# Entering the attention core of a two-block training kernel: the row shift by Ln and Exp, its last quarter inside the core, and q's second half stored in four pieces

## The chip, the cores and the metric

The kernel runs on one core of a Trainium2 chip. The metric is the time of one execution in microseconds, read on the device. Nine runs of the kernel before gave a median of 1085.01 us (1078.76 to 1089.26).

## The reference

Two small attention blocks are run forward and backward on 2048 tokens of width 448 with 16 heads of 28. Block A is linear attention, block B has one key and value head for all 16 query heads. The outputs are the forward result of both and all eight gradients. What matters here is block B:

```python
q = (x @ wq).reshape(B, S, H, Dh).transpose(0, 2, 1, 3)
k, v = x @ wk, x @ wv
p = softmax(einsum("bhqd,bkd->bhqk", q, k) * Dh ** -0.5)
o = einsum("bhqk,bkd->bhqd", p, v)
out_B = o.transpose(0, 2, 1, 3).reshape(B, S, H * Dh) @ wo
_out, _vjp = jax.vjp(_fwd, A_x, ..., B_wo)
_grads = _vjp(grad_out)
```

A softmax may subtract any number of its own from each row. The kernel subtracts the bound |q| * max|k|, the square root of |q|^2 * max|k|^2, which is called the shift. It is stored as row 0 of each head's group of 32 rows in q (28 of the others are the head's values), and k has -1 in that row, so that the matmul of q and k delivers the shifted score.

## The kernel before, in words

The program has three stages.

**Phase A** (to about 194 us) does block A. **Phase B** (`phase_B_pre`, 194 to 223 us) forms k, v and q of block B, and the shifts. **The core** (223 to about 1010 us) runs forward and backward of block B's attention together. A tail forms the remaining gradients. In the first two stages a planner orders the instructions of each engine; the core is under `tc.manual_schedule()`, where each engine's order is the program's.

Phase B goes over q in four chunks of 512 tokens (`qc`). For each, TensorE makes four groups of 128 rows (L571), ScalarE copies them into `R1`, which is `qT` (L572), VectorE squares them (L574), and TensorE sums the squares by head into `pn` (L577). Then ScalarE takes the square root with the scale `kmax2` (L579) into `shifts[qc]`, a part of the tile `ga` for the first three chunks and of `R3` for the last. Four small DMAs on GpSimd's queue write the 16 rows into `R1` (L581). After every second chunk, SyncE's queue issues four DMA transposes of 1024 tokens of `R1` into `qn` (L586; `qn` is the tile `gaT`) and one store of 1 MB to `qn_d` in DRAM (L587). The core reads `qn_d` back in an order of its own (`qX`).

The core goes over 64 blocks of 256 queries by 2 heads, each in 8 units `u` of 256 keys, so 512 units and 28 more that drain the pipeline. A unit computes scores into `sps` (two PSUM banks of three in `SB`) and exponentiates them on ScalarE into `eT` (L891 and L931). From unit 16 on the backward step of unit `u - 16` runs beside it: `dps` (two banks, `DB`) is multiplied by `eT` on VectorE (L896), and, after a copy `cp` on ScalarE (L898), on GpSimd (L899), which gives `dsT`. Every fourth unit, one DMA transpose on SyncE's queue makes `eN` from four units of `eT` (L933, 1 MB). The gradient of v (`dv_mm`) reads `eN` from unit 20 on. The gradient of k (`dk_m`) reads `qX` from unit 27 on. The 256 KB of `qX` that a range of 8 blocks needs come in four loads on GpSimd's queue (L904), where `a` is a group of 32 partitions: for the first range at units 10, 14, 18 and 22, for the second at 34, 42, 50 and 58. In units 1 to 15 TensorE also projects the output gradient (`do_proj`, evicted on VectorE at L866).

Memory is taken from pools. `cA` holds nearly all working tiles of phases A and B (`xa`, `ga`, `pq`, `ppB` and others), `cB` only `gaT`, `awk` some small ones, and `psA` the eight PSUM banks, four each under the names `aacc` and `agen`. All four close at L605, and the core's pools are laid over the same memory: `eT`, `eN`, `dsT` and one `qX` buffer over `cA`, the other `qX` buffer (`pqb_`) over `cB`, `dsx` over both. A pool that lies over a closed one waits for it: the first instruction on each engine that touches a tile of the new pool carries the waits.

## Time and profile before

| | |
|---|---|
| median of 9 runs | 1085.01 us (1078.76 to 1089.26) |
| the profiled execution | 1085.64 us, of which the span of the trace is 1083.9 us |
| granted TensorE clock, mean over the span | 0.992 |
| busy: TensorE, ScalarE, VectorE, GpSimd | 1035.3 (96%), 875.7 (81%), 894.6 (83%), 772.4 (71%) us |
| table loads on ScalarE | three of 1.28 us: at the start, at L579 (207.5 us), at L870 (222.5 us) |
| first and last exponential of the core, L891 | start at 223.93 and 1006.97 us |
| one unit in the steady core | 1.46 us (median distance of the L891 starts) |

How to read it: a line of the profile names start, duration, engine, line, operation, output and inputs; a bracket holds the idle time of the engine before it and what ended that. TensorE's share is that of issued work and not of its peak. The program is the same in the nine runs, which are not profiled.

### The profile page before, as it was taken

To read this page: it belongs to the slowest core of one execution; us is meant where nothing else is said; L and a number is where in the kernel's file an instruction comes from. 1 tells how busy PE (TensorE), PEld (TensorE's weight loads), DVE (VectorE), ACT (ScalarE), POOL (GpSimd) and SP (SyncE) were. 2 spreads that over 40 slices of the span, in tenths; PEclk is the share of its full clock that TensorE was granted. 3 is DMA by queue.
4 is the path that set the end of the run, shared out by engine and by line. 5 is a ranking of instruction groups with operands and counts; after the bars stand their busy time and mean duration, and the time that the engine had idled before them with its cause. 6 is when DMAs were issued, how large, how long until landed. Compare 5 with 4: busy or idle time off the path is not lost.

```text
span 1083.9 us, 40115 instructions
## 1 busy us (share of the span) xinstructions
PE 1035.3 (96%) x16326; PEld 494.3 (46%) x16329; DVE 894.6 (83%) x1790; ACT 875.7 (81%) x1743; POOL 772.4 (71%) x1014
## 2 busy tenths in 40 slices
PE   9999999998999999999999999999999999999998
PEld 5555555443444444444444444444444444444434
DVE  6887400437999999999999999999999999999942
ACT  6453122577999999999999999999999999999621
POOL 6001143226888888889888888988988899888881
PEclk9999999989999999999999999999999999999999
DMA  9869899399999999999999999999999999999973
GB/s 237 161 124 195 166 188 213 63 212 160 200 185 195 199 209 190 191 192 195 195 179 191 197 197 190 203 187 187 187 205 186 191 198 189 192 180 180 224 133 90
DMA packets 669026, 199.36 MB, mean 184 GB/s; under 512 B 646008, under 2 KB 664736, under 8 KB 668840
## 3 DMA queue, kind: packets, MB, share of 16 engines
q1 hardware_dynamic: 656296, 175.23, 97.0%
q0 software_dynamic: 7584, 17.59, 6.8%
q10 hardware_dynamic: 4960, 3.96, 1.3%
q8 instruction: 128, 2.10, 0.8%
q14 instruction: 58, 0.48, 0.1%
HBM read 20.99 MB, written 12.94 MB: 31 GB/s over the span
## 4 chain that ended last, share of the span: by engine, by line
PE 39%; ACT 19%; POOL 15%; DVE 13%; issue 10%; DMA 4%; ACTq 0%; DVEq 0%; POOLq 0%; SPq 0%
PE agen L81 13%; POOL dsT L899 11%; ACT cp L898 10%; ACT eT L931 7%; PE sps L640 6%; DVE dsx L962 5%; PE oq L640 5%; PE aacc L81 5%; DVE dsT L896 3%; PE sps L81 3%; PE dv_acc L640 2%; DMA eN<-eT 1%; PE dk_acc L640 1%; PE dps L640 1%; POOL prod L787 1%
## 5 line engine op out<-in xcount | busy, mean ns | idle before, releaser
L899 POOL TENSOR_TENSOR dsT<-cp,eT 128x512 bf16<-128x512 bf16 x512 | 588.6, 1157 | 103.2 <-ACT cp L898 97.5
L962 DVE STREAM_TRANSPOSE dsx<-dsT 128x512 f32<-128x512 f32 x512 | 357.9, 699 | 2.4 <-DVE ot L710 0.2
L640 PEld LDWEIGHTS <-R 128*32 128x32 bf16 (+1 forms) x9184 | 229.7, 94 | 276.7 <-issue 237.0
L896 DVE TENSOR_TENSOR dsT<-dps,eT 128x512 bf16<-128x512 f32 x512 | 341.8, 668 | 15.9 <-PE dps L640 11.1
L891 ACT ACTIVATE eT<-sps 128x512 bf16<-128x512 f32 x512 | 312.6, 611 | 23.4 <-PE dps L640 10.0
L898 ACT ACTIVATE cp<-dps 128x512 bf16<-128x512 f32 x512 | 314.2, 614 | 12.0 <-PE dps L640 10.9
L931 ACT ACTIVATE eT<-sps 128x512 bf16<-128x512 f32 x512 | 320.3, 626 | 0.0
L640 PE MATMUL dk_acc<-dsx,qX 32*32 32x512 bf16 x4096 | 269.4, 376 | 2.9 <-DMA qX<-qn_d 2.9
L640 PE MATMUL dps<-doT,R 32*128 32x256 bf16 x2048 | 248.4, 269 | 1.9 <-ACT cp L898 0.8
L640 PE MATMUL sps<-R,R 32*128 32x256 bf16 (+1 forms) x2240 | 222.6, 274 | 7.8 <-DVE R L866 1.7
L640 PE MATMUL oq<-eT,R 128*32 128x256 bf16 x2048 | 158.5, 276 | 0.0
L640 PE MATMUL oq<-dsT,R 128*32 128x256 bf16 x2048 | 156.9, 275 | 0.1
L640 PEld LDWEIGHTS <-qX 32*32 32x32 bf16 x4096 | 80.1, 89 | 118.5 <-issue 55.4
L640 PE MATMUL dv_acc<-eN,don 128*32 128x512 bf16 x1024 | 97.7, 381 | 1.0 <-DMA eN<-eT 1.0
L81 PEld LDWEIGHTS <-R 128*128 128x128 bf16 (+1 forms) x525 | 42.1, 100 | 40.8 <-issue 11.0
L401 POOL COPY pk<-R 128x256 bf16<-128x256 bf16 x4 | 1.6, 398 | 75.3 <-DVE R L361 66.1
L553 DVE TENSOR_TENSOR osb<-R 32x512 bf16<-32x512 bf16 x4 | 1.6, 412 | 59.0 <-ACT R L550 59.0
L640 PEld LDWEIGHTS <-don 128*32 128x32 bf16 x1024 | 33.9, 97 | 2.2 <-issue 1.6
L787 POOL TENSOR_TENSOR prod<-R,oTs 128x128 f32<-128x128 bf16 x64 | 28.0, 437 | 9.3 <-DVE oTs L783 8.9
L916 DVE TENSOR_SCALAR R<-oq 64x256 bf16<-64x256 f32 x64 | 27.3, 427 | 3.6 <-PE oq L640 1.6
L804 PE MATMUL sps<-identB,don 128*32 128x128 bf16 x256 | 18.5, 222 | 12.3 <-POOL don L796 8.0
L81 PE MATMUL agen<-R,R 128*128 128x448 bf16 x128 | 28.8, 354 | 0.2 <-ACT R L220 0.2
(223 smaller groups left out, 987.5 us busy)
## 6 DMA issues: line engine op xcount, KB each, us to landing
qX<-qn_d POOLq DMA_DIRECT2D x32, 256.0 KB, 4.6
out_dram<-osb ACTq DMA_DIRECT2D x22, 112.0 KB
qn_d<-gaT SPq DMA_DIRECT2D x2, 1024.0 KB
eN<-eT SPq DMA_TRANSPOSE x128
xa<-in_A_x_dram SPq DMA_DIRECT2D x8, 224.0 KB
ga<-in_grad_out_dram SPq DMA_DIRECT2D x4, 448.0 KB
xa<-in_grad_out_dram POOLq DMA_DIRECT2D x4, 448.0 KB, 9.0
out_dram<-wdq POOLq DMA_DIRECT2D x8, 224.0 KB, 4.5
```

What stands on the lines that cost most here:

```text
L81: nc.tensor.matmul(out_ap, lhsT=lhsT, rhs=rhs, start=start, stop=stop, tile_position=(0, 0))
L401: nc.gpsimd.tensor_copy(out=pk[:, t4, D:512], in_=gqn[:, t4, 3 * P:D])
L640: nc.tensor.matmul(out, lhsT=lhsT, rhs=rhs, start=start, stop=stop, tile_position=pos, skip_group_check=True)
L787: nc.gpsimd.tensor_tensor(out=prod[b][:], in0=dnv, in1=os_, op=ALU.mult)
L804: nc.tensor.transpose(tp2[q:q + 32, qb * P:(qb + 1) * P], don[b][:, qb, h, :], identB[:, :], tile_position=(0, q))
L891: nc.scalar.activation(out=eT(u)[:, 0, :], in_=sp[0][:, :], func=ACT.Exp, scale=scale)
L896: nc.vector.tensor_tensor(out=dst[:, 0, :], in0=dp[0][:, :], in1=ew[:, 0, :], op=ALU.mult)
L898: nc.scalar.activation(out=cp[:, :], in_=dp[1][:, :], func=ACT.Copy)
L899: nc.gpsimd.tensor_tensor(out=dst[:, 1, :], in0=cp[:, :], in1=ew[:, 1, :], op=ALU.mult)
L916: nc.vector.tensor_scalar(out=qT_B[g][64 * hp:64 * hp + 64, qc * 256:(qc + 1) * 256], in0=oq[64:128, 0:256], scalar1=scale, scalar2=None, ...
L931: nc.scalar.activation(out=eT(u)[:, 1, :], in_=sp[1][:, :], func=ACT.Exp, scale=scale)
L962: nc.vector.transpose(out=dsx[b][:, tp, :, :, :].rearrange("p h t c -> p (h t c)").bitcast(F32), in_=dsT[y][:, :, :].rearrange("p h c -> p ...
```

## The change

The square root becomes `Ln` and `Exp`: `exp(0.5 * ln(kmax2 * pn + 1e-30))`, first in place in PSUM, then into the shift. The dummy activation at the core's entry (L870) goes. For the last chunk of 512 tokens this step and its four small DMAs are moved into the core, behind the first exponential of unit 1. The first half of `qn` is kept in eight rows of `ppB` (pool `cA`) in place of `gaT` (pool `cB`). The second half is transposed at the core's start into the buffer of `qX` that lies in `pqb_`, and is stored by tokens in four pieces of 256 KB on GpSimd's queue at units 34, 42, 50 and 58; the second range of `qX`, which uses that buffer next, is loaded at units 66, 70, 74 and 78, and `wo` at 86 in place of 70. The PSUM pool `psA` stays open, and the core's banks are taken from its two names.

```diff
@@ phase_A @@
-        return xbT, wq_pad, rep, bsel, gaB, ga[:, 8:12, :]
+        return xbT, wq_pad, rep, bsel, ppB[:, 6:14, :], ga[:, 8:12, :]
@@ phase_B_pre @@
-            shift = shifts[qc]
-            nc.scalar.activation(out=shift, in_=pn[0:H, :], func=ACT.Sqrt, scale=kmax2[:, 0:1])
-            for g in range(4):
-                nc.gpsimd.dma_start(qT[:, g, qs].rearrange("(j r) s -> j r s", r=32)[:, 0, :], shift[4 * g:4 * g + 4, :])
-            if qc % 2:
-                q2 = slice((qc - 1) * 512, (qc + 1) * 512)
-                t2 = slice(4 * qc - 4, 4 * qc + 4)
+            if qc == NQC - 1:
+                break
+            q_shift(pn, shifts[qc], qs)
+            if qc == 1:
                 for g in range(4):
-                    nc.sync.dma_start_transpose(qn[:, t2, g * P:(g + 1) * P], qT[:, g, q2])
-                nc.sync.dma_start(qn_d[q2, :].rearrange("(t p) c -> p t c", p=P), qn[:, t2, :])
+                    nc.sync.dma_start_transpose(qn[:, :, g * P:(g + 1) * P], qT[:, g, 0:1024])
+                nc.sync.dma_start(qn_d[0:1024, :].rearrange("(t p) c -> p t c", p=P), qn)
+    def q_shift(pn, shift, qs):
+        nc.scalar.activation(out=pn[0:H, :], in_=pn[0:H, :], func=ACT.Ln, bias=eps[:, 0:1], scale=kmax2[:, 0:1])
+        nc.scalar.activation(out=shift, in_=pn[0:H, :], func=ACT.Exp, scale=0.5)
+        for g in range(4):
+            nc.gpsimd.dma_start(R1[:, g, qs].rearrange("(j r) s -> j r s", r=32)[:, 0, :], shift[4 * g:4 * g + 4, :])
@@ between the stages @@
+    psc = ExitStack()
+    psA = psc.enter_context(tc.tile_pool(name="psA", bufs=4, space=bass.MemoryType.PSUM))
     with ExitStack() as pa:
-        psA = pa.enter_context(tc.tile_pool(name="psA", bufs=4, space=bass.MemoryType.PSUM))
-        phase_B_pre(pa, cA, awk, psA, io)
+        last_shift = phase_B_pre(pa, cA, awk, psA, io)
-        SB = [psA.tile([P, 512], F32, name=f"sps{i}") for i in range(3)]
-        DB = [psA.tile([P, 512], F32, name=f"dps{i}") for i in range(2)]
+        SB = [psA.tile([P, 512], F32, name="aacc") for i in range(3)]
+        DB = [psA.tile([P, 512], F32, name="agen") for i in range(2)]
+        oq, dk_acc = (psA.tile([P, 512], F32, name="agen") for _ in range(2))
@@ the core's loop @@
-            tc.keep_in_program_order(nc.scalar.activation(out=ex[:], in_=ex[:], func=ACT.Exp))
+            qn = pqb_.tile([P, 8, 512], BF16, name="qX")
+            for g in range(4):
+                nc.sync.dma_start_transpose(qn[:, :, g * P:(g + 1) * P], R1[:, g, 1024:2048])
...
+                if u == 1:
+                    q_shift(*last_shift)
+                    dv_acc = psA.tile([P, 512], F32, name="aacc")
...
-                for a in {10: (0,), 14: (2,), 18: (1,), 22: (3,)}.get(u, ()) or {34: (0,), 42: (2,), 50: (1,), 58: (3,)}.get(u % 64, ()) * (u < 448):
-                    qc = u // 64 + (u > 24)
+                for n in {34: (0,), 42: (1,), 50: (2,), 58: (3,)}.get(u, ()):
+                    nc.gpsimd.dma_start(qn_d[1024 + 256 * n:1280 + 256 * n, :].rearrange("(t p) c -> p t c", p=P),
+                                        qn[:, 2 * n:2 * n + 2, :])
+                for a in {10: (0,), 14: (2,), 18: (1,), 22: (3,), 66: (0,), 70: (2,), 74: (1,), 78: (3,)}.get(u, ()) or {
+                        34: (0,), 42: (2,), 50: (1,), 58: (3,)}.get(u % 64, ()) * (96 < u < 448):
+                    qc = u // 64 + (u > 96)
...
-                if u == 70:
+                if u == 86:
                     nc.gpsimd.dma_start(wo, wo_d[:, 0:D].rearrange("(g p) c -> p g c", p=P))
```

`kmax2` and the constant `eps` are moved to the pool that lives to the end.

## The prediction

> **What bounds the kernel now.** I read the page first: over the span TensorE is 96% and ScalarE 81% busy, an average over stages. The distances of the L891 starts then give the pace of the core: 1.46 us a unit from about unit 30 on, with ScalarE 99% busy in stretches of 100 us (its three activations of a unit start about 0.49 us apart). Nothing that the change touches lies on that pace, except GpSimd's queue. What is left is the entry, 205 to 275 us, so I asked for busy times in stretches cut where the granted clock changes (columns: length, busy and count of TensorE, its weight loads, VectorE, ScalarE, GpSimd, then clock, DMA share, GB/s).
>
> ```profile
> 222.00:225.50 3.50, 1.44 (x13) 0.71 (x14) 0.63 (x1) 3.47 (x7) 2.75 (x7) 1.00 0.60 133
> 225.50:232.30 6.80, 6.80 (x44) 2.65 (x42) 1.70 (x4) 3.72 (x7) 0.59 (x1) 0.50 1.16 235
> 232.30:246.70 14.40, 14.17 (x140) 7.07 (x137) 6.29 (x17) 11.30 (x22) 1.83 (x5) 1.00 1.19 236
> ...
> 252.80:256.20 3.40, 2.36 (x50) 1.02 (x43) 2.35 (x6) 2.17 (x5) 3.18 (x6) 1.00 0.80 174
> ...
> 263.10:266.50 3.40, 1.73 (x33) 0.84 (x33) 3.33 (x8) 2.89 (x6) 3.03 (x6) 1.00 1.23 150
> 266.50:273.30 6.80, 5.30 (x61) 1.78 (x65) 2.05 (x5) 2.04 (x4) 2.19 (x3) 0.50 1.27 185
> ```
>
> Twice a stretch of 3.4 us in which TensorE was busy for 41% and 51% is followed by 6.8 us at half clock; the stretch with 69% is not. Units 1 to 15 are bound by TensorE (full but for 0.2 us in the third row), so the first half clock costs about 3.4 us.
>
> The waits from 246 to 275 us name what stopped TensorE (total, times, longest):
>
> ```profile
> PE dk_acc L640 <- DMA qX<-qn_d: 2.9, 1, 2.9
> PE dv_acc L640 <- DMA eN<-eT: 1.0, 1, 1.0
> ```
>
> The timeline of the entry shows who stands around it:
>
> ```profile
> 222.52 1.28 ACT L870 ACT_TABLE_LOAD   x1
> ...
> 222.79 2.24 POOL L581 DMA_DIRECT2D R<-R  x4 [0.20 <-issue]
> 223.82 0.20 ACT L870 ACTIVATE ex<-ex 128x1 f32<-128x1 f32 x1
> 223.93 0.58 ACT L891 ACTIVATE eT<-sps 128x512 bf16<-128x512 f32 x1
> 223.95 0.36 SPq L587 DMA_DIRECT2D qn_d<-gaT  x1
> ```
>
> ScalarE's first exponential follows the table load; SyncE issues the first half's store at the same moment. And ScalarE at the two waits:
>
> ```profile
> 255.49 0.60 ACT L891 ACTIVATE eT<-sps 128x512 bf16<-128x512 f32 x1 [1.23 <-PE dps L640]
> ...
> 264.82 0.60 ACT L891 ACTIVATE eT<-sps 128x512 bf16<-128x512 f32 x1 [0.40 <-PE dps L640]
> ...
> 270.45 0.60 ACT L891 ACTIVATE eT<-sps 128x512 bf16<-128x512 f32 x1 [4.05 <-PE dps L640]
> ...
> 272.83 0.60 ACT L891 ACTIVATE eT<-sps 128x512 bf16<-128x512 f32 x1 [0.81 <-PE dps L640]
> ```
>
> Unit 20 (252.67 to 255.49) takes 2.82 in place of 1.47 us: 1.35 lost. Units 27 to 29 (264.82 to 274.39) take 9.57 in place of 4.41 us: 5.2 lost, 3.2 of them until the fourth qX load lands at 267.95 by the trace's landing events, 2.0 by the half clock behind it. Unit 26 loses 0.3. These 6.85 us, the half clock and the table load are all that the entry has to give back.
>
> The DMA issues say why the load is late (issues, KB, median us to landing), first for 225 to 275 us, then for 375 to 910:
>
> ```profile
> qX<-qn_d POOLq DMA_DIRECT2D x4, 256.0 KB, 8.0
> ```
> ```profile
> qX<-qn_d POOLq DMA_DIRECT2D x24, 256.0 KB, 4.2
> ```
>
> Early in the core SyncE's transposes are behind: eN of units 16 to 19, ready at 252.8, is issued at 262.6, and the lag is gone only near 400 us.
>
> **The change, part by part.** The sum is made against the profiled execution, 1085.64 us (span 1083.9 and 1.74 around it); the median of the runs is 0.63 lower.
>
> *The new wait.* As compiled, the kernel before puts twenty semaphore conditions ahead of the first L891. Among them are the shift DMAs that read `ga`, the transposes of L93 that read `xa`, and the L495 store of `kv`: none of these shares an address with `eT`'s first buffer, all are tiles of `cA`. The stores from `gaT` (`cB`) are not among them, but stand in front of the first L898 and L962, whose buffers lie over `cB`. So a core pool waits for the whole pool beneath it. The change puts the first half of `qn` into `ppB`, which is in `cA`: the first exponential now waits for the store of 1 MB to land. Before, that store was issued at 223.95 and landed at 229.1 by the landing events. It comes 0.5 us later (next item), and the conditions behind it on ScalarE take about 0.4 (six pairs from 223.17 to 223.66 before). So L891 starts at about 230.0 in place of 223.93: +6.0, between +5.4 (nothing added to the landing) and +6.6. Queued behind it is every activation of the core, and TensorE, with three score banks, waits for those.
>
> *Ln and Exp.* L579 took 0.68 us. Ln I take at the same; Exp lies between the 0.20 of the 128x1 Exp at L870 and the 0.60 of an L891 of equally many columns, and I take 0.60. ScalarE needs 4 x 0.60 + 0.68 + 0.60 = 3.7 us a chunk beside 4.5 us of TensorE (217.29 to 221.83 from one L579 to the next), so TensorE hides it; uncovered it would be 3 x 0.60 = 1.8. On the way to the first half's transposes it isn't hidden: +0.6, less about 0.1 since the table load at 207.5 no longer delays the chunk. Both removed loads (1.28 each) bring nothing: the first lies beside TensorE, which was busy 3.89 of 4.00 us there, the second now lies beside the store. For a load the trace shows 1.28 us and the next activation directly behind it. "ScalarE: Activation LUTs" of the Trainium skill, What ACT_TABLE_LOAD costs, counts about 2.66 us with a drain; by that, two loads would free 5.3 us in place of 2.6, and the sum is the same by both, as nothing waits for them any more.
>
> *The last shift inside unit 1.* 1.3 us of ScalarE, with the second exponential of unit 1 queued behind, which unit 2's `oq` matmuls need. TensorE, at half clock, has two projections (0.97 us each in the chain at half clock) and two rounds of scores (0.54) before it needs that: 3.0 us, against 2.8 on ScalarE. Between 0 and 1.3; I take 0.2. Its four GpSimd DMAs (0.56 each) must not overwrite `R1` before the second half's transposes have read it (landed at 237.1 before). Behind them stand the first `qX` load and the work on `prod` of unit 10, which comes at 239.66 + 6: hidden. With an undelayed entry it would cost up to 0.6.
>
> *The second half.* Its four transposes stay where they were on SyncE (224.50 and after). The 1 MB store leaves that queue: 3.2 us between the landings of the first `eN` (240.58) and the store (243.76). On GpSimd the pieces take 0.73 us each (the stores of L505) at units where loads of 0.58 stood, and four loads move to units 66 to 78: 2.3 us more in 16 units of about 24.8 us, in which GpSimd (86% busy from 350 to 450 us) has 3.5 free. Cost 0, up to 2.3 if that is gone. A second-range load has 13 units to land. The open PSUM pool lets TensorE start 0.8 us earlier (222.69, released by L592), which nobody can use.
>
> *The clock.* TensorE is now idle from 222.6 to 230.6, so the half clock comes in any case. Before it lasted for 7.8 us of work (224.56 to 232.3); behind one to two full stretches of 3.4 us, and what is left of the first, it would be 3.4 to 10.2: -2.2 to +1.2, I take 0. "TensorE: Matmul & The Clock Gate", Part 1, lets the clock fall after an idle window of about 3.4 us and rise after a busy one. The rows show a fall at 41% busy already. By the page the gap of before would have cost nothing and this longer one costs 1.7 to 3.4 us; the sum by it would be some 2.5 us higher.
>
> *What is repaid.* With the entry 6 us later and 3.2 us of transfers gone, `eN` of units 4 to 7, ready at about 242, is no longer behind the store; unit 20 doesn't wait: -1.35, and unit 26 -0.3. The fourth `qX` load has 5.5 us (259.22 to 264.75). It now meets a shorter lag, but four loads still fall into 12 units: I take 7.0 us, between 4.2 and 8.0 and nearer to 8.0. That leaves a wait of 1.5 for 3.2, and half of the clock's 2.0: 2.7 of the 5.2 are repaid (0 to 5.2).
>
> Sum: 6.0 + 0.2 + 0 - 1.35 - 0.3 - 2.7 = +1.9, so 1087.5 for a run like the profiled one, and **1087.0** against the median.
>
> **The rivals.** *Not repaid (slower).* One mechanism: the fourth `qX` load still takes what it took. Against it speaks the shorter lag; for it, that loads of 256 KB took 6.2 to 10.9 us in seven of the first eight cases. At 8.7 us the 5.2 stay: 6.2 - 1.65 = +4.6, at 10.9 +6.8. It decides from about 8.2 us on, and gives 1090.5.
>
> *No wait for the store (faster).* If the core's pools waited by address, the first exponential would start at about 222.4 (scores from 221.95), 1.5 earlier; the gap of TensorE would be about 0.5 us and the clock would stay (3.4). The transposes then set the end of the entry, and they are relieved by the store's 3.2 us alone, less 0.5: about -3, and 1081.5. Against it stand the conditions listed above.
>
> *The two functions don't share a table set (it doesn't do what it says).* Then each Ln and each Exp loads one: 2.6 us more a chunk, ScalarE 6.3 against 4.5, 1.8 x 3 = 5.4, and 2.6 more ahead of the store: +8 on top, 1095.
>
> **How the numbers follow.** A measurement of this kernel can tell about 0.3% (3.3 us) from no change. The forecast has 0.54 (0.44 of it within 0.3%, 0.08 slower, 0.02 faster), with a range of its own of 1083 to 1090.5; not repaid 0.28 (0.24 slower); no wait 0.13 (0.11 faster); two tables 0.05. Faster 0.13, same 0.50, slower 0.37. The range reaches to 1081.5, which takes in half of the third case, and to 1091.5, which takes in most of the second.
>
> **What would show it.** First L891 at about 230 us and ScalarE idle for some 8 us before it; one table load in the kernel; TensorE idle from 222.6 and half clock until 234 to 240; no `eN` wait at unit 20; a `qX` wait under 2 us at unit 27; the same 1.46 us a unit behind unit 90. A first exponential before 225 us, or a second stop of TensorE of 4 us, would prove me wrong.

## The result, and the profile after

The changed kernel takes **1102.74 us** (median of 10 runs, 1100.57 to 1104.08) where the kernel before took 1084.36 (median of 31 runs beside it, 1078.76 to 1093.79): slower, ratio **1.0166**, 95% interval 1.0146 to 1.0187. The forecast was 1087.0 with a range from 1081.5 to 1091.5.

The page of the profile after, its span and the line of busy times:

```profile
span 1100.3 us, 40113 instructions
...
PE 1037.2 (94%) x16326; PEld 492.2 (45%) x16329; DVE 895.4 (81%) x1790; ACT 885.8 (81%) x1752; POOL 774.2 (70%) x1018
```

TensorE has 2 us more of work than before and ScalarE 10: the rest of the loss is waiting. The timeline of the entry, ScalarE's lines (the lines of L579 are now L594 for Ln and L595 for Exp, L891 is L894):

```profile
205.21 1.28 ACT L594 ACT_TABLE_LOAD   x1
206.51 0.73 ACT L594 ACTIVATE aacc<-aacc,eps,kmax 16x512 f32<-16x512 f32 x1
...
207.77 1.28 ACT L595 ACT_TABLE_LOAD   x1
209.06 0.59 ACT L595 ACTIVATE ga<-aacc 16x512 bf16<-16x512 f32 x1
...
230.78 0.60 ACT L894 ACTIVATE eT<-aacc 128x512 bf16<-128x512 f32 x1 [7.93 <-DMA qn_d<-pqpT]
...
231.87 0.60 ACT L894 ACTIVATE eT<-aacc 128x512 bf16<-128x512 f32 x1
232.48 1.28 ACT L594 ACT_TABLE_LOAD   x1
233.78 0.73 ACT L594 ACTIVATE aacc<-aacc,eps,kmax 16x512 f32<-16x512 f32 x1
234.52 1.28 ACT L595 ACT_TABLE_LOAD   x1
235.82 0.59 ACT L595 ACTIVATE R<-aacc 16x512 bf16<-16x512 f32 x1
236.31 0.57 ACT L941 ACTIVATE eT<-aacc 128x512 bf16<-128x512 f32 x1
```

Two things are to be seen. Every Ln and every Exp has a table load of its own ahead of it, so the kernel has nine loads and not one; two of them stand in unit 1, between its two exponentials, which are 4.4 us apart. And the first exponential waited 7.93 us, in the end for the store of the first half, as forecast.

The busy times in stretches cut where the clock changes (columns as in the prediction):

```profile
222.00:226.90 4.90, 2.19 (x40) 1.34 (x40) 2.52 (x5) 0.86 (x2) 2.56 (x7) 1.00 0.89 154
226.90:247.40 20.50, 14.28 (x83) 5.29 (x82) 3.20 (x8) 12.41 (x20) 2.82 (x5) 0.50 0.76 154
...
274.70:278.10 3.40, 0.72 (x11) 0.21 (x10) 2.32 (x5) 1.72 (x4) 3.02 (x5) 0.99 1.31 101
278.10:284.90 6.80, 3.88 (x45) 1.33 (x45) 1.39 (x3) 1.43 (x3) 0.27 (x1) 0.50 1.21 183
```

Half clock lasts 20.5 us at the entry, where it lasted 6.8; the second one is as before. The wait of TensorE between 240 and 290 us, ScalarE's exponentials of units 27 and 28, and the landing times of the first four loads of `qX` (those that the L914 line issues before 300 us):

```profile
PE agen L641 <- DMA qX<-qn_d: 5.5, 1, 5.5
```
```profile
275.24 0.60 ACT L894 ACTIVATE eT<-aacc 128x512 bf16<-128x512 f32 x1 [0.40 <-PE agen L641]
...
283.47 0.60 ACT L894 ACTIVATE eT<-aacc 128x512 bf16<-128x512 f32 x1 [6.65 <-PE agen L641]
```
```profile
DMA to landing us min/median/max: 3.3/8.4/11.3
```

The wait for `eN` is gone, but the one for `qX` has grown from 2.9 to 5.5 us, though the entry is later: the fourth load is issued at 269.65 and lands 11.3 us later.

**Where the time went.** Absolute times of two traces must not be set against each other here: phase A varies from run to run. ScalarE's first copy of phase B starts at 195.59 us in the trace of before and at 193.28 in that of after, and anywhere from 192.9 to 199.4 in the 18 traces of this study, in no order by kernel. Counted from that copy on:

| stretch | before | after | difference |
|---|---|---|---|
| phase B, first to last copy of q (L572) | 16.57 | 20.86 | +4.29 |
| last copy of q to the first exponential | 3.62 | 8.50 | +4.88 |
| units 0 and 1 | 2.04 | 6.01 | +3.97 |
| units 2 to 15 | 20.74 | 21.38 | +0.64 |
| units 16 to 26 | 18.11 | 17.07 | -1.04 |
| units 27 to 31 | 12.55 | 14.64 | +2.09 |
| units 32 to 95 | 99.15 | 100.38 | +1.23 |
| units 440 to 451 | 18.46 | 21.24 | +2.78 |
| all else behind phase A | | | -0.1 |
| sum | | | **+18.7** |

The medians differ by 18.4. All experiments below are read in the same stretches; "unit 0" is the start of the first exponential counted from that first copy of phase B, and "over before" is the difference to the median of the kernel before in the same set of runs. That median lay between 1083.49 and 1085.32 us from set to set, so plain differences between the times of two kernels below hold to a microsecond or two, and "over before" is the better measure. The stretches of a row are those of one profiled execution each, which can lie off its kernel's median: that of "before, Ln and Exp, one set" is the longest of its twelve (1093.14, median 1086.01), that of "both, last shift in phase B" the shortest (1081.30, median 1088.43), and the form without the wait and with its loads on GpSimd has no row, since its only trace is 7 us above its median.

| kernel | over before | ratio, 95% interval | unit 0 | units 2-15 | 16-26 | 27-31 | from 32 on |
|---|---|---|---|---|---|---|---|
| before | | | 28.3 | 20.7 | 18.1 | 12.6 | 806.6 |
| **after** | +18.4 | 1.0166 [1.0146, 1.0187] | 37.5 | 21.4 | 17.1 | 14.6 | 810.5 |
| after, one set | +5.0 | 1.0052 [1.0030, 1.0074] | 34.4 | 20.0 | 17.1 | 10.1 | 809.4 |
| after, half in `cB` | +5.7 | 1.0067 [1.0033, 1.0101] | 33.3 | 19.1 | 17.1 | 8.3 | 809.6 |
| after, both | +3.8 | 1.0034 [1.0009, 1.0058] | 29.4 | 18.2 | 19.8 | 11.5 | 810.2 |
| before, Ln and Exp, two sets | +7.0 | 1.0057 [1.0036, 1.0078] | 34.3 | 22.4 | 17.1 | 13.2 | 806.3 |
| before, Ln and Exp, one set | +2.5 | 1.0026 [1.0006, 1.0045] | 29.6 | 19.5 | 19.6 | 12.8 | 807.8 |
| after, loads at unit 0 | +10.5 | 1.0084 [1.0057, 1.0111] | 37.5 | 21.4 | 16.8 | 7.4 | 811.4 |
| after, clock kept up | +12.2 | 1.0118 [1.0096, 1.0141] | 37.4 | 18.4 | 17.1 | 7.7 | 811.6 |
| both, loads at unit 0 | +4.5 | 1.0034 [1.0003, 1.0065] | 29.7 | 22.9 | 18.0 | 7.4 | 810.7 |
| both, pieces on SyncE | -0.5 | 1.0009 [0.9979, 1.0040] | 29.6 | 21.9 | 17.1 | 10.7 | 806.7 |
| both, last shift in phase B | +3.1 | 1.0014 [0.9983, 1.0045] | 29.5 | 19.3 | 17.1 | 7.4 | 809.5 |
| both, pieces on SyncE, shift in B | +2.1 | 1.0002 [0.9981, 1.0023] | 29.5 | 20.4 | 17.1 | 7.3 | 810.4 |
| before, loads of `qX` on SyncE | -1.6 | 0.9994 [0.9976, 1.0013] | 28.4 | 20.5 | 16.9 | 16.5 | 801.2 |
| after, loads of `qX` on SyncE | +4.8 | 1.0054 [1.0036, 1.0072] | 37.4 | 22.5 | 16.8 | 7.4 | 803.9 |
| four parts undone, loads on SyncE | -3.3 | 0.9965 [0.9950, 0.9981] | 29.8 | 19.5 | 16.8 | 13.3 | 802.0 |
| no wait, early loads, on SyncE | **-9.9** | **0.9914** [0.9894, 0.9933] | 27.8 | 20.8 | 17.0 | 7.3 | 801.8 |

### The profile page after: what moved, and what is told of

It reads as the page before. It is cut to its first block, busy times and chain, and to the rows that moved or that the text cites. A ratio compares the mean times of both kernels' runs of the same rounds, so it can differ in the third digit from the quotient of the medians.

```text
span 1100.3 us, 40113 instructions
## 1 busy us (share of the span) xinstructions
PE 1037.2 (94%) x16326; PEld 492.2 (45%) x16329; DVE 895.4 (81%) x1790; ACT 885.8 (81%) x1752; POOL 774.2 (70%) x1018
## 4 chain that ended last, share of the span: by engine, by line
PE 37%; ACT 20%; POOL 17%; DVE 12%; issue 11%; DMA 2%; ACTq 0%; SPq 0%; DVEq 0%; POOLq 0%
PE agen L82 13%; POOL dsT L905 12%; ACT cp L904 10%; ACT eT L941 8%; PE aacc L82 7%; PE agen L641 7%; PE aacc L641 7%; DVE dsx L972 5%; DVE dsT L902 3%; ACT eT L894 1%; POOL prod L788 1%; POOL don L791 1%; PE aacc L805 1%; DMA qX<-qn_d 1%; DVE R L926 1%
## 5 line engine op out<-in xcount | busy, mean ns | idle before, releaser
L902 DVE TENSOR_TENSOR dsT<-agen,eT 128x512 bf16<-128x512 f32 x512 | 341.8, 668 | 18.3 <-PE agen L641 13.6
L894 ACT ACTIVATE eT<-aacc 128x512 bf16<-128x512 f32 x512 | 313.0, 611 | 36.3 <-PE agen L641 14.3
L904 ACT ACTIVATE cp<-agen 128x512 bf16<-128x512 f32 x512 | 315.1, 615 | 12.0 <-PE agen L641 12.0
L941 ACT ACTIVATE eT<-aacc 128x512 bf16<-128x512 f32 x512 | 321.5, 628 | 0.0
L641 PE MATMUL agen<-dsx,qX 32*32 32x512 bf16 x4096 | 269.7, 377 | 5.5 <-DMA qX<-qn_d 5.5
L641 PE MATMUL agen<-doT,R 32*128 32x256 bf16 x2048 | 249.1, 269 | 2.2 <-DVE dsT L902 1.1
L641 PE MATMUL aacc<-R,R 32*128 32x256 bf16 (+1 forms) x2240 | 223.1, 275 | 12.9 <-ACT eT L894 6.7
L641 PE MATMUL agen<-eT,R 128*32 128x256 bf16 x2048 | 159.3, 276 | 1.7 <-ACT eT L941 1.7
L641 PE MATMUL agen<-dsT,R 128*32 128x256 bf16 x2048 | 157.1, 275 | 0.1
L641 PE MATMUL aacc<-eN,don 128*32 128x512 bf16 x1024 | 97.7, 382 | 0.0
L82 PE MATMUL agen<-R,R 128*128 128x448 bf16 (+1 forms) x188 | 40.7, 348 | 0.1
L788 POOL TENSOR_TENSOR prod<-R,oTs 128x128 f32<-128x128 bf16 x64 | 27.9, 436 | 11.9 <-DVE oTs L784 11.5
L805 PE MATMUL aacc<-identB,don 128*32 128x128 bf16 x256 | 18.5, 222 | 14.6 <-POOL don L797 10.7
```

The source lines that it names most:

```text
L82: nc.tensor.matmul(out_ap, lhsT=lhsT, rhs=rhs, start=start, stop=stop, tile_position=(0, 0))
L641: nc.tensor.matmul(out, lhsT=lhsT, rhs=rhs, start=start, stop=stop, tile_position=pos, skip_group_check=True)
L788: nc.gpsimd.tensor_tensor(out=prod[b][:], in0=dnv, in1=os_, op=ALU.mult)
L805: nc.tensor.transpose(tp2[q:q + 32, qb * P:(qb + 1) * P], don[b][:, qb, h, :], identB[:, :], tile_position=(0, q))
L894: nc.scalar.activation(out=eT(u)[:, 0, :], in_=sp[0][:, :], func=ACT.Exp, scale=scale)
L902: nc.vector.tensor_tensor(out=dst[:, 0, :], in0=dp[0][:, :], in1=ew[:, 0, :], op=ALU.mult)
```

## The experiments

### The two causes seen in the trace, one by one and together

The table loads taken out: one instruction at the head of the changed kernel.

```diff
+    nc.scalar.preload_act_table_set("natural_log_exp_and_others")
     R1 = reg.tile([P, 4, S], BF16, name="R1")
```

> The changed kernel with one instruction more, at its head: a load of the table set that holds natural logarithm, exponential and copy together. Theory 1 (the two functions were given two sets): one table load in the whole kernel instead of nine. In phase B and ahead of the store six loads of 1.28 us go; two or three of them lay on the way to the end of phase B (it ended 2.3 us later than before), so the first L894 (here L895) starts at 228 to 229 instead of 230.8. In unit 1 two loads go, 2.6 us of ScalarE between its two exponentials. Time 5 to 7 us below the changed kernel: 1095.5 to 1098. Rival (the loads hide behind TensorE and behind the wait for the store): the store still goes out after 225 and the time stays within 1.5 us of 1102.7. Rival (clock): the long half clock (20.5 us from 226.9) comes from the loads in unit 1; without them it is under 10 us and the time falls by 9 or more.

Measured: 1088.90 us, 13.8 less than the changed kernel. Its timeline:

```profile
228.51 0.60 ACT L895 ACTIVATE eT<-aacc 128x512 bf16<-128x512 f32 x1 [8.85 <-DMA qn_d<-pqpT]
...
230.08 0.72 ACT L595 ACTIVATE aacc<-aacc,eps,kmax 16x512 f32<-16x512 f32 x1
230.83 0.59 ACT L596 ACTIVATE R<-aacc 16x512 bf16<-16x512 f32 x1
```

There is one load in the kernel (at 0.81 us), and Ln and Exp of unit 1 stand directly behind each other. Theory 1 has its parts right: phase B's copies take 16.84 us (4.0 less), units 0 and 1 take 3.29 (2.7 less: two loads), and the wait for the store stays. But the time fell by more than its 5 to 7: units 2 to 15 give 1.4, with 13.7 us at half clock in place of 20.5, and units 27 to 31 another 4.5.

The store's wait taken out: the first half of `qn` back in the pool where it was.

```diff
-        return xbT, wq_pad, rep, bsel, ppB[:, 6:14, :], ga[:, 8:12, :]
+        return xbT, wq_pad, rep, bsel, gaB[:, 0:8, :], ga[:, 8:12, :]
```

> The changed kernel with the first half of qn in the buffer gaT of pool cB, as in the kernel before, and nothing else different. Theory 1 (ScalarE's first exponential waits for the store because the store reads pool cA): the first L894 starts when phase B ends, at 225.5 to 226.5 instead of 230.8, and the pool of the second half (over cB) waits for the store in its place; time 4 to 5 us below the changed kernel: 1097.5 to 1099. Rival (what the wait gave up is taken back at units 20 to 28, by the eN and qX waits, as the prediction had it for half of it): the first L894 starts as early but the time falls by at most 2.5 us. Rival (another thing of the entry holds the first exponential, the shifts' transfers on GpSimd's queue or the shared PSUM pool): it starts within 1 us of 230.8.

```profile
226.87 0.60 ACT L894 ACTIVATE eT<-aacc 128x512 bf16<-128x512 f32 x1 [3.71 <-DMA R<-ga]
```

The store is issued at 225.97 and no longer what the first exponential waits for: the pool was the cause. Unit 0 comes 4.2 us earlier, as expected, but the time falls by 13.1 to 1089.63, where 4 to 5 was expected. Here too the rest comes behind it, 2.3 in units 2 to 15 and 6.4 in units 27 to 31. Four of the twelve executions took 1096 to 1100.5 and the other eight 1087 to 1090.3, so in this kernel the late loss comes and goes.

Both edits together:

> Both of the two edits together: one table set, loaded once at the head, and the first half of qn in pool cB. Theory 1 (table loads and store wait are the whole loss): the first L895 starts at 223 to 224.5, unit 16 within 2.5 us of the kernel before, and the time within 3 us of it: 1084 to 1088. Rival (a part of the loss is neither: the fourth of the loads of qX at units 10 to 22 lands late, 11.3 us after its issue, the pieces of the second store, or the stall of 3 us at units 445 to 447): the first L895 starts as early, but the time stays 4 to 7 us over the kernel before, 1088.5 to 1091.5.

1087.70 us, so 13 by one edit, 13 by the other, 15 by both. The time lies in Theory 1's range, 1084 to 1088; over before it is +3.8, between the two expectations, and its interval (1.0 to 6.3 us) takes in both. The stretches decide for the rival, that a part is neither: 3.6 us more than before are needed from unit 32 on, where neither edit acts, and all forms of the changed kernel with pieces and loads on GpSimd's queue need 809.4 to 811.6 us there, before and its two forms 806.3 to 807.8. Unit 0 starts 8.1 us before that of the changed kernel, but now 19.8 us are needed for units 16 to 26 (`eN` is late) and 11.5 for units 27 to 31. Each single edit gave back a third thing as well, most of which lies at unit 27, and it can be given back only once.

The same loads in the kernel before, whose last shift is in phase B:

```diff
-            nc.scalar.activation(out=shift, in_=pn[0:H, :], func=ACT.Sqrt, scale=kmax2[:, 0:1])
+            nc.scalar.activation(out=pn[0:H, :], in_=pn[0:H, :], func=ACT.Ln, bias=eps[:, 0:1], scale=kmax2[:, 0:1])
+            nc.scalar.activation(out=shift, in_=pn[0:H, :], func=ACT.Exp, scale=0.5)
```

> The kernel before with one edit: its four square roots of the shift are each an Ln and an Exp (times 0.5), all in phase B, with the table sets as they fall (two loads for each, nine in all). Theory 1: each chunk holds 2.6 us more of loads and 0.6 more of work on ScalarE, of which the last chunk's 3.9 lies open ahead of its transposes and of the other three only what the changed kernel showed, 2.3; the first L891 (here L893) starts 3 to 5 us later than 223.9 and the time is 3 to 5 us over the kernel before: 1087.5 to 1089.5. Rival (the loads hide behind TensorE in phase B, only those in unit 1 cost): the first L893 within 1.5 us of 223.9 and the time within 2 us.

+7.0 us: phase B's copies take 20.86 us, exactly as in the changed kernel, and 1.7 more lie between the last copy and the first exponential. Theory 1 expected 3 to 5 and is short: the first exponential comes 6.0 us later, and units 2 to 15 take 22.4 us, 1.6 more than before, with 17.1 us at half clock. The same with one set:

> The kernel before with its square roots as Ln and Exp, and one table set for the whole kernel, loaded at its head. Against the kernel before it is without the two loads of 1.28 us at 207.5 and 222.5 and has 0.6 us more of ScalarE a chunk; against the run with two sets it is without eight loads. Theory 1 (what those cost, 7 us, was all the loads): time within 1.5 us of the kernel before. Rival (the load at 222.5, just ahead of the first exponential, was on the path): the first exponential starts at 222 to 223 and the time is 1.5 to 3 us under the kernel before.

+2.5 us: the eight loads were worth 4.5 of the 7.0. Nothing is left of a gain by Ln and Exp: without the load that the kernel before had ahead of its first exponential, that exponential waits 1.67 us for a transfer and comes no earlier (unit 0 at 29.6 against 28.3). The prediction had it that removing this load brings nothing.

### What happens at unit 27

The first four loads of `qX` in the changed kernel, moved:

```diff
-                for a in {10: (0,), 14: (2,), 18: (1,), 22: (3,), 66: (0,), 70: (2,), 74: (1,), 78: (3,)}.get(u, ()) or {
+                for a in {0: (0, 2, 1, 3), 66: (0,), 70: (2,), 74: (1,), 78: (3,)}.get(u, ()) or {
```

> The changed kernel with the first four loads of qX issued at unit 0 instead of at units 10, 14, 18 and 22; table loads and store wait as they are. What stood after the first runs: either of the two edits alone gave back about 13 us, both together 15, so the two losses don't add; in the changed kernel the fourth load of qX landed 11.3 us after its issue, against 6.6 to 8.4 with an edit, and TensorE stood 5.5 us for it at unit 27. Theory 2 (most of what is beyond the two waits, 4 to 6 us, is this late landing): unit 27 takes under 3 us instead of 8.2 and the time falls by 4 to 6 us, to 1096.5 to 1098.5. Rival (the transposes of eN set that pace by themselves, whatever the loads do): a wait for eN takes its place and the time falls by under 2 us. Rival (half clock alone makes the difference): no change at unit 27 and the time within 1 us.

1095.79 us, 7.0 less. Ahead of unit 16 nothing has changed, unit 0 and units 2 to 15 to a tenth; units 27 to 31 take 7.4 us instead of 14.6. So 7 us of the loss are the late fourth load. The same edit on both corrections:

> One table set, first half of qn in cB, and the first four loads of qX at unit 0. In the run of both edits the waits at units 20, 22 and 27 (for eN and qX) took some 6 us beyond the pace, though the first exponential started at 223.5. Theory 2: without loads among the eN transposes these waits go: unit 28 at 263.5 to 266 instead of 268.9, and the time 3 to 5 us under that of both edits, 1083 to 1085. Rival (the loads collide with the four transposes of the second half and the first eN instead): the eN wait at unit 20 stays at 1 us or more and the time is within 1.5 us of 1087.7.

1089.86 us, no gain: the rival, though it is 2.2 us longer and not within 1.5. Here the second half's transposes wait for the store (they use the buffer over `cB`), the four loads run among them and the first `eN`, and units 2 to 15 take 22.9 us with a half clock of 10.2 us from 246.5. The loads cost less in one place and more in another.

The clock, with all waits left in place: 24 matmuls whose results nothing reads.

```diff
+            for _ in range(16):
+                mm(dk_acc[:, :], identB[:, :], kT_rep[:, 0:512])
             for u in range(NU + 28):
...
                 if u == 1:
+                    for _ in range(8):
+                        mm(dk_acc[:, :], identB[:, :], kT_rep[:, 0:512])
                     q_shift(*last_shift)
```

> The changed kernel, with table loads and store wait as they are, and 24 matmuls of 128x512 more whose results nothing reads: 16 while TensorE waits for the first exponential (its idle stretch of some 6 us from 224.5), 8 in unit 1 while ScalarE works at the last shift. Theory 3 (the long half clock, 20.5 us from 226.9, is a cost of its own): half clock lasts under 10 us, units 2 to 16 take 18.2 to 19.5 us instead of 21.4, and the time falls by 2 to 6 us, to 1097 to 1100.5. Rival (the landing of the fourth load of qX sets when unit 28 starts, whatever the clock before it): units 2 to 16 are as much shorter but unit 28 starts within 1.5 us of 283.5 and the time stays within 1.5 us of 1102.7. Rival (the clock follows the light load of units 0 to 8, not the idle stretch ahead of them): half clock stays at 17 us or more and nothing changes.

```profile
224.50:232.50 8.00, 5.38 (x55) 2.66 (x55) 1.94 (x4) 0.23 (x1) 1.93 (x6) 1.00 0.94 237
232.50:239.30 6.80, 6.12 (x23) 2.27 (x22) 0.42 (x1) 6.64 (x10) 0.86 (x2) 0.50 0.45 78
```

1095.73 us, 7.0 less. The first row, with the idle stretch now 67% busy, stays at full clock; half clock falls to 6.8 us. Unit 0 starts as late as before the edit, units 2 to 15 take 18.4 instead of 21.4 us, and units 27 to 31 take 7.7: with units 2 to 15 in 18.4 us, the fourth load, issued at the same unit 22, landed after 6.1 us. So half clock cost 3.0 us by itself here, and with it went 6.9 at unit 27. (1.3 of these 9.9 are lost again in units 0 and 1 and from unit 32 on; counted from phase B, the two traces differ by 8.7.) "TensorE: Matmul & The Clock Gate" of the Trainium skill, Part 1, lets the clock rise after one busy window of about 3.4 us. The changed kernel's trace differs; the last 10.6 us of its half clock:

```profile
236.80:247.40 10.60, 10.47 (x63) 3.91 (x62) 2.35 (x6) 6.46 (x13) 2.71 (x5) 0.50 0.76 127
```

TensorE is busy for 10.47 of them, three such windows, and the clock is still at half.

### GpSimd's queue

The four pieces of the second store, on both corrections, issued by SyncE:

```diff
-                    nc.gpsimd.dma_start(qn_d[1024 + 256 * n:1280 + 256 * n, :].rearrange("(t p) c -> p t c", p=P),
+                    nc.sync.dma_start(qn_d[1024 + 256 * n:1280 + 256 * n, :].rearrange("(t p) c -> p t c", p=P),
```

> Both edits, and the four pieces of the second store issued by SyncE instead of GpSimd. GpSimd's issue of a piece takes 0.78 us, that of a load of qX 0.58, and units 32 to 64 took 50.6 us in every form of the changed kernel against 49.9 before. Theory (GpSimd's time is on the way there, so its 0.2 us more each is lost four times): units 32 to 64 take 47.5 to 49.9 us, time 0.7 to 3 us under that of both edits; and the stall of GpSimd of 1.3 us ahead of the load at unit 442, found in all forms of the changed kernel and not before, moves or goes, for another 2 us, if it hangs on how many instructions GpSimd has had. Rival (the transfers themselves slow the eN transposes, whoever issues them): units 32 to 64 stay at 50.6 us and the time within 1 us.

1084.85 us, 2.9 less (4.3 by "over before"; the two intervals overlap, so the stretches have to decide). Units 32 to 63 take 49.3 us (both corrections 50.6, before 49.9), and units 440 to 451 take 18.44 us instead of 20.44. In the second stretch every form that has the pieces and the loads on GpSimd's queue loses 2.0 to 3.2 us against before. In the changed kernel's timeline GpSimd stalls there, ahead of the load of unit 442:

```profile
918.61 0.58 POOL L914 DMA_DIRECT2D qX<-qn_d  x1 [1.30 <-issue]
```

Its 1.3 us stop GpSimd where it has no slack, and TensorE then waits for `don`, which GpSimd makes (waits from 915 to 932 us: total, times, longest):

```profile
PE aacc L805 <- POOL don L797: 1.2, 1, 1.2
```

With the pieces on SyncE this stall is not there, nor, further down, with the loads on SyncE and the pieces on GpSimd (18.3 us). That it hangs on what GpSimd had issued is shown; what it is isn't.

The last shift back in phase B, on both corrections:

```diff
-            if qc == NQC - 1:
-                break
             q_shift(pn, shifts[qc], qs)
...
                 if u == 1:
-                    q_shift(*last_shift)
```

> Both edits, and the last chunk's shift back in phase B, ahead of the core. Theory (the shift in unit 1 costs its 1.3 us of ScalarE there, in phase B it lies ahead of the last transposes, which wait for the store anyway): unit 1 takes 1.1 us instead of 2.2, the first exponential starts 0 to 1 us later, and the waits at units 20 to 27 take back what is left: time within 1 us of both edits, 1086.7 to 1088.7. Rival (the first exponential waits for the transfers of the last shift, over 2 us): it starts at 226 or later and the time is 1.5 to 3 us longer.

1088.43 us, within 1 us as expected, but in two groups: four executions from 1081.3 to 1083.2 and eight from 1086.6 to 1092. The profiled one is of the first: no stop at unit 27, where the fourth load landed 4.5 us after its issue. With both, pieces on SyncE and the shift in phase B:

> One table set, first half in cB, pieces issued by SyncE, last shift in phase B: all four parts that were found to cost, undone together. The pieces on SyncE gave back 1.3 us at units 32 to 64 and 2.0 at units 440 to 452; the shift in phase B gave a run without a stop at unit 27 in some executions (1081 to 1083) and the old time in others. Theory: the two add, 1078 to 1085, a little under the kernel before. Rival (the waits for eN and qX at units 20 to 28 take it back, as between both edits and either of them): 1084 to 1087.

1085.61 us, in the rival's range of time, but not by its cause: in its trace no unit from 20 to 28 stops. The entry is as good as any, unit 32 starts 20 us earlier than in the changed kernel when counted from phase B's start, and yet the time is that of before: units 64 to 95 take 53.0 us instead of 49.7. The DMA issues of 35 us there, first in this kernel, then in that with the pieces on SyncE alone (issues, KB, median us to landing):

```profile
qX<-qn_d POOLq DMA_DIRECT2D x4, 256.0 KB, 9.9
...
eN<-eT SPq DMA_TRANSPOSE x5
```
```profile
qX<-qn_d POOLq DMA_DIRECT2D x4, 256.0 KB, 4.2
...
eN<-eT SPq DMA_TRANSPOSE x7
```

The same four loads, at the same units; they land after 7.3 to 13.1 us in the slower one and after 3.8 to 4.6 in the other, and five transposes are issued in place of seven. In the slower one SyncE issues its transposes 3 us behind the units (`eN` of units 60 to 63 at 322.86, unit 64 at 319.89; in the other 0.15 us behind), and the loads fall into the middle of them. A form without any wait for the store, its tiles of `eT` taken in the reverse order and its pool waiting tile by tile, with the loads at unit 0:

```diff
-        return xbT, wq_pad, rep, bsel, gaB[:, 0:8, :], ga[:, 8:12, :]
+        return xbT, wq_pad, rep, bsel, ppB[:, 6:14, :], ga[:, 8:12, :]
-        pe_ = cs_.enter_context(tc.tile_pool(name="ceT", bufs=1, side="right"))
+        pe_ = cs_.enter_context(tc.tile_pool(name="ceT", bufs=1, side="right", reuse_waits="tile"))
-        ETs = [pe_.tile([P, 4, 2, 512], BF16, name=f"eT{i}") for i in range(5)]
+        ETs = [pe_.tile([P, 4, 2, 512], BF16, name=f"eT{i}") for i in range(5)][::-1]
```

> As the last, with the first half of qn again in pool cA, but with the pool of eT waiting tile by tile (and its tiles taken in the reverse order, so that the one which overlaps the stored buffer is used last), so that neither the first exponential nor the transposes of the second half wait for the store; and the first four loads of qX at unit 0. Theory 2 (loads at the entry helped by 7 us where the second half's transposes were already through, and not where they waited for the store): the first exponential starts at 223 to 224, unit 28 at 262 to 265, and the time is 1077 to 1081. Rival (the loads collide with the first eN transposes whatever the order): units 8 to 16 take over 13 us instead of 10.7, and the time is 1083 to 1087.

1084.99 us (ratio 1.0004, 0.9978 to 1.0029): by time the rival. Its sign, over 13 us for units 8 to 16, is not in the one trace there is (10.7).

### One queue for both

What was left was a load of `qX` on GpSimd's queue beside a transpose on SyncE's. All loads of `qX` go to SyncE, in line with the transposes; the edit is the same in four kernels.

```diff
-                    nc.gpsimd.dma_start(qX[qc][32 * a:32 * a + 32, :, :, :].rearrange("j b s c -> j b (s c)"),
+                    nc.sync.dma_start(qX[qc][32 * a:32 * a + 32, :, :, :].rearrange("j b s c -> j b (s c)"),
```

In the changed kernel:

> The changed kernel with nothing different but the queue of the qX loads, SyncE's instead of GpSimd's. Theory 4: the first exponential as late as before (230.8) and half clock as long, but the fourth load lands within 8 us, unit 27 takes under 4 us instead of 8.2, and the time falls by 4 to 9 us, 1094 to 1099. Rival (bytes): unit 27 as long as it was, time within 2 us of 1102.7.

1088.45 us, **14.3 less** by this edit alone (4 to 9 were expected), with all nine table loads, the wait for the store and 23.9 us of half clock still there. Units 27 to 31 take 7.4 us, and from unit 32 on it needs 803.9 us instead of 810.5. In the kernel before:

> The kernel before with nothing changed but the queue of the qX loads, SyncE's instead of GpSimd's. Theory 4: the stops at units 20 (1.35 us) and 27 to 28 (5 us) shrink, and units 32 to 64 take 49.3 us instead of 49.9; 1074 to 1080. Rival (bytes): stops of the same size, time within 2 us of the kernel before. Rival (SyncE becomes the bound, since it spends 5 of 5.9 us on each transpose and would have 0.4 to 0.6 more): units get longer behind unit 32 and the time is 3 us or more over the kernel before.

1082.00 us: in time the rival, within 2 us and not to be told from no change. In the stretches it is both. From unit 32 on it gains as much (801.2 against 806.6), but units 27 to 31 take 16.5 us: with the second half's transposes and store ahead of them in the same line, the loads come later. What is gained in the steady core is another thing than the meeting of load and transpose. The unit four behind each load (102 for the load at 98) is shorter, by 0.10 to 0.21 us on the mean, which makes 3.9 us over the 24 loads of units 98 to 442. TensorE waited there for `don`, which GpSimd finishes a few instructions behind its 0.58 us for the load's issue. The waits for it from 280 to 1000 us, first in the kernel before (total, times, longest; PEld is TensorE's weight load), then in this one:

```profile
PEld L804 <- POOL don L796: 18.8, 41, 0.7
PE sps L804 <- POOL don L796: 8.0, 26, 0.4
```
```profile
PEld L804 <- POOL don L796: 5.9, 28, 0.2
```

TensorE's 26 waits are gone. In the changed kernel with the same edit, which keeps the four pieces on GpSimd's queue, three are left, 1.4 us. The edit does two things at once, then: a load no longer runs beside a transpose, and GpSimd no longer issues it. In the form with all four parts undone:

> All four costly parts undone and the loads of qX by SyncE, at the units where they were. Theory 4: units 64 to 96 take 49.3 instead of 53.0 us and the time is 1073 to 1079. Rival (bytes): still over 51 us there, time within 3 us of 1085.6.

1080.34 us, 5.3 less than with the loads on GpSimd, and just above the 1079 of Theory 4; units 64 to 95 take 49.5 us. But units 27 to 31 take 13.3 us in place of 7.3: here too the loads come later in the line. And in the form without the wait and with the loads at unit 0:

> The last run (no wait for the store, loads at unit 0) with all loads of qX issued by SyncE, in line with the transposes of eN. Theory 4 (a load on GpSimd's queue that runs beside a transpose slows both; in one line they don't meet): no stop in units 16 to 28 or 64 to 96 (the latter 49.3 us or less), and GpSimd free of 28 issues of 0.58 us; time 1070 to 1077. Rival (the bytes are what costs: the transposes alone fill the DMA engines, a load delays the next transpose by as much in line): units 64 to 96 stay over 51 us and the time within 3 us of 1085.

**1073.70 us, faster than the kernel before: ratio 0.9914, 0.9894 to 0.9933.** The stretch of units 27 to 31, first here, then in the kernel before (columns as above):

```profile
262.80:270.20 7.40, 7.28 (x140) 3.31 (x137) 7.25 (x14) 7.34 (x15) 6.48 (x10) 1.00 1.20 203
```
```profile
264.80:277.40 12.60, 9.56 (x139) 3.53 (x137) 7.48 (x14) 7.72 (x16) 6.47 (x10) 0.73 1.19 182
```

The same instructions of the engines, here with TensorE 98% busy at full clock; the four loads are through by then. "DMA: Bandwidth & Descriptors" of the Trainium skill, SWDGE vs HWDGE vs iDMA, sends plain copies to SyncE or ScalarE and leaves GpSimd the irregular ones; these runs agree, with 14.3 us in one kernel, 11.3 and 5.3 in two others, and 1.6, not to be told from nothing, in the kernel before. Whether any queue but GpSimd's would do, or it must be the one of the transposes, no run here shows: ScalarE's was not tried.

## Why the prediction was wrong

Step by step, with the terms of its sum (+1.9) against the measured +18.7 of the traces:

- **The new wait** (+6.0, of which 0.5 for Ln and Exp). Right in cause and nearly in size: +4.88 between the last copy of q and the first exponential, and the kernel with the half in `cB` has no such wait. The rival without it is out.
- **"Ln and Exp share a set" is the step that failed first.** The prediction counted one table load in the kernel and took the removed loads as worth nothing; it named the case in which the two don't share a set at 0.05. Nine loads were there. With one set the changed kernel takes 1088.90 us, inside the range of the forecast, so these loads and what hung on them (13.4 us by "over before") are enough to take the time out of it. The price of that rival, 1.8 us for each of three chunks, 5.4, is near the 4.29 measured in phase B. Its other 2.6, ahead of the store, did not show (the store goes out 3.4 us behind the last copy of q, before 3.6), and it left out the two loads in unit 1, where 3.97 us were lost in place of 0.2 (2.7 by the loads, as the run with one set shows, and 1.25 by Ln and Exp themselves, near the upper bound of 1.3 given). Ln took 0.73 us and Exp 0.59, about what was taken. "ScalarE: Activation LUTs", Table sets: the hidden batching unit, counts one load for a logarithm followed by an exponential, since one set holds both. That set exists and one load is enough, as the run with it shows; but as compiled, nine loads were there, alternating. A set that could be shared was taken for a set that would be. Even the rival's 1095 was 8 us short, by the two loads in unit 1 and by the last two items below.
- **The clock** (0). Against the kernel before it is +0.64, since that had a half clock too. In absolute terms half clock lasted 20.5 us, twice the longest case of the prediction, and the run that kept it up shows that 3.0 us hung on it in units 2 to 15 and 6.9 behind them.
- **What is repaid** (-1.65 and -2.7) is the second step that failed: it had the wrong sign where it was largest. Units 16 to 26 gave back 1.04, by unit 20 alone; unit 26 had nothing to give, as it takes 2.01 us in both traces. Units 27 to 31 lost 2.09 more, 4.8 from the forecast, because the fourth load landed after 11.3 us and not after 7.0; the bounds, 4.2 to 8.0, were too narrow although the prediction itself knew of 10.9. *Not repaid* was the rival that came true here, on top of the one with two sets. It decided, as it said, from a landing of 8.2 us on.
- **The second half** (0, up to 2.3). +1.23 in units 32 to 95: GpSimd's issues are on the pace there, four pieces of 0.75 to 0.78 us in place of four loads of 0.58. And +2.78 at units 440 to 451, 2.0 or more in every form with pieces and loads on GpSimd's queue, which no row of before shows.

Of what would show it right, no `eN` wait at unit 20 and the same pace of the core came (the median distance of the L891 and L894 starts is 1.48 us in both traces; the 1.46 given ahead is a little low). The first exponential at about 230 (230.78) is luck: phase A ended 2.3 us earlier in this trace, and counted from phase B it came 9.2 us later than before, where 6.1 was forecast. One table load, half clock until 234 to 240 and a `qX` wait under 2 us did not come, and TensorE's stop of 5.5 us at unit 27 is one of the two signs that it named as proof against it. Two slips changed nothing: by its own terms "no wait" gives 1082 and not 1081.5, and the last six pairs of conditions start at 223.02.

**What stays open.** Why the fourth load, issued at unit 22 in all of them, took 11.3 us in the changed kernel and 7.2, 6.6 and 6.1 with one set, the half in `cB` or the clock kept up. Loads that ran among transposes landed late, and the transposes fell behind with them; moving the loads to unit 0 or to SyncE's queue ended the stop at unit 27 in the changed kernel. But which overlap gives 11 us and which 7 was not found, nor why loads in SyncE's line leave 16.5 and 13.3 us in units 27 to 31 of two kernels and 7.4 in the changed one. How much of the gain from that queue is the meeting and how much is GpSimd's time is separated only in the steady core, where it is GpSimd's time. And the stall of GpSimd at unit 442 has no cause yet.

## What to carry to other kernels

Before a function is replaced by two, look in the compiled program whether the table loads are one or alternate; an explicit load of a set that holds both, at the head of the kernel, was worth 13.8 us here. When a stretch ends with the landing of a transfer, an earlier start of the stretch need not end it earlier: single corrections then overlap (13 and 13 gave 15), and the transfer itself must be tried, its place and its queue. An engine that only issues a transfer pays for the issue, and where it is on the pace the next engine waits for it. Compare two traces from an event that both have, not from the start of the run.

## What the runs showed of the hardware that was not expected

- A load of 256 KB on GpSimd's queue landed after 3.6 to 5.8 us in the steady core of the kernel before, where transposes run too, and after 7.3 to 13.1 us at units 66 to 78 of the form whose transposes were 3 us behind; there the transposes slowed as well, five in 35 us in place of seven.
- The issue of such a load took GpSimd 0.58 us, and TensorE waited for GpSimd 26 times, 8.0 us in all, between 280 and 1000 us of the kernel before; with the loads on SyncE's queue these waits were gone, and those of its weight loads fell from 18.8 to 5.9 us. The core from unit 32 on then needed 801 to 804 us, in four kernels, where the rows with the loads on GpSimd's have 806 to 812.
- Phase A, the same in all kernels, ended anywhere between 192.9 and 199.4 us. Whether that also makes the spread between executions of one kernel is not shown, as there is one trace of each.
- A table load took 1.28 us and the activation behind it started 1.30 us after the load's start (205.21 to 206.51, to 0.01), in all eight cases of phase B and unit 1.
- Half clock went on for 10.6 us (236.8 to 247.4 in the changed kernel) while TensorE was 99% busy.
